# Two chained attention kernels on one core: more turning on TensorE, four experts scored densely in the last two batches

## The chip, the core and the metric

One core of one Trainium2 chip runs the whole program. The metric is the device time of one execution in microseconds (us), median of three.

## What is computed

Eight batches (B), eight heads (H), 512 tokens (S) and 32 state rows (Ns) of 64 numbers (D). First every head lets its tokens read the state and the state read the tokens. The 544 resulting rows, heads side by side, are the input (512 wide) of a mixture of four attention experts, of which each row takes two:

```python
scores = scale * x @ state.T ; xread = softmax(scores) @ state          # per batch and head
scores2 = scale * state @ x.T ; sread = softmax(scores2) @ x
y = concat([xread, sread], axis=2)                                      # -> (8, 544, 512)
topk = two largest of y @ w_gate ; w = softmax over the two
for e in range(4):
    q, k, v = y @ wq[e], y @ wk[e], y @ wv[e]
    ye = softmax(causal(scale * q @ k.T)) @ v @ wo[e]
    out += (w of e where e is chosen, else 0) * ye
```

(The reference pads the rows to 576 in a setup that isn't used; the output has 8 x 544 rows of 512.)

## The kernel before

Nearly all numbers are held as a pair of float16, a high part and the rest, and a product of two such numbers is three float16 matmuls (`PROD`, high by high, high by low, low by high). `hi_lo` (L356) and `split` (L338) make the pairs.

Per batch there are these steps, each a function inside the kernel. `load` (L503) fetches x. `front` (L527) splits x into a float16 pair (`xh`), turns it (`xT`, by a DMA transpose issued on SP's queue; batch 0 turns it on TensorE before the split and splits the turned values), scores it against the state (`bd`), takes the softmax in `eb`, turns that into `at`, folds the state into the weights (`gs`), and from `at` and `gs` makes values `v`, gate logits `lg`, keys `kt` and queries. `gate` (L809) finds the two chosen experts. The queries of a tile of 128 tokens are written twice with masks: one slot holds the chosen lower expert, the other the chosen higher one, each as three experts' columns of which two are zeroed (`qf`); split to `qh`, they are turned by a DMA transpose into `qm`. `side` (L776) does the state's read of the tokens (`e2`, `a`, `a2t`), and every second batch `tail` (L962) handles the 64 state rows of two batches.

`probs` (L843) takes a unit of one or two of the four token tiles: scores of both slots (each three wide matmuls over two experts' 128 rows and three narrow ones over one expert's 64 rows; two narrow ones run side by side in the array), mask and maximum on VectorE (`masked`), exponential on ScalarE, split, and a DMA transpose of the pair (`pt<-ph`). `reads` (L886) multiplies with the values (two slots, three experts each, 193 columns), divides, weights, adds the slots, splits (`zh`), turns by one DMA transpose a tile (`z<-zh`; the last batch's three smaller tiles on TensorE), multiplies with `wo` and sends 128 rows out. Units are `[(0, 1), (2,), (3,)]` for each batch (L1069); a unit is read two units later (`LAG`).

What the code records is not the order on the engines. Every operation becomes a step (`Steps.step`, L175), and `Steps.run` (L256) issues all of them in the order of the table `ORDER`, worked out ahead; the same table holds, for steps that may run on several engines (`either`, L210), which one it is, and which buffer each use takes. So all instructions carry line L266, and only tile names tell them apart. Each engine works through its list in order, and all DMAs are issued by SP, in order too. `FILL` (L19) places 34 matmuls on zeros in the first 15 us (`warm`, L498); their operand is called `band`.

Of the kernel before, what the change touches and what calls it, by code (L numbers as in the profile page):

```python
# [11 lines left out]
F32 = mybir.dt.float32  # L12
# [6 lines left out]
CFG = dict(FILL=(1.0, 1.4, 1.8, 2.2, 2.6, 3.0, 3.4, 3.8, 4.2, 4.6, 5.0, 5.4, 5.8, 6.2, 6.6, 7.0, 7.4, 7.8, 8.2, 8.6, 9.0, 9.4, 9.8, 10.2, 10.6, 11.0, 11.4, 11.8, 12.2, 12.6, 13.0, 13.4, 13.8, 14.2,), RA=-1, RG=1, RV=2, RK=2, ZL=3, GP=1, PT=4, ZM=4, SM=4, QM=4, SIDE=32, FB=1, PX=1, PA=2, LB=1, xn=4, W0=-33, PACE=37.0, LAG=2,  # L19
           FRONT=1.5, FSPAN=1.0, TSPAN=1.3, TOFF=1.2, KT=3, p32=3, ph=2, at=1, et=1, gs=1, xh=4, a2=1, o=4, sn=1, qf=2,  # L20
           n_eb=1, n_e2=1, n_a2t=1, n_xt_tail=2, n_z32=3, n_z=2, n_zh=3, n_tq=1, n_tv=2, n_tpt=2, n_tz=2)
ORDER = (
    (
        "c-jq@gO(5q6acSpwbf>8+ict0X4|%Hd$VoZwr$(Cjraax&Y77ikPPxdQb-B;AQ(zQey9)0p%8>(L)Z-f2m}lQ3I+}tAq(t<RFD<+K_<ussi8"
        "5Xhs=-`!a;b5009sYvO^=-18E=^<bZV00&+u6D2nAV543~|*b17!UFZx~p*3`YI#3tdKqV{z_n-_^g$!^Xib7W?2c_U3Jb<=P3<^LBs09z99"
        "Xy3d5E%j?3PgoIPz}1lV`vYLpgVMczR(Q%!4oKh(I7g+fS3>qVnZB=3-KU6bcCAF1A0Pb>;;{mIF!WU@C*t<b0~{Vp*MuWC3p_?U^EngvhV^"
        "9K^1%nwV^sxf>KxvC%{Rl4A<Zl6vsGp9!lUTNB{{T5hRBGa2Q_0Bp3r@;V7JeBQOHSK}8${17IMWgNYCZAut#g!v#17Q(*>7gCQ^zPQxr157"
        "XfUEP?ef8|J`Sm<#)19$bW_P!89^P?!%3U?D7m)vyM(KxupfTVWe)fMxI&*1;{<4kIBhZG;2x4vxbpsD_(x2W*0>cpJ9iPS^~?U^8yV9XJ`P"
        "<8qh+v1kj{z^!-(8saXfiLG%3G{T+O0ItAF2+zB)7QTnw*ckWVDo6rB@CBM+3fhacu|1}wBy=4vLkDb%!4yOtu?{9A!XHo<Q_**5gJ0nre1M"
        "<u8=7G<`UUkcDgA{26s(Voe;_$E$3(Ob|3L#(bnJwQX+O5W8vmo#8M|Q@Y>5Z3Eq2B3*aKT(KWvBP!7w65;KBF_`r`l$hlug0Cw_+bG!(;Q0"  # L30
# [239 lines left out]
def state_read_then_moe_attention(ctx: ExitStack, tc: tile.TileContext, x, state, w_gate, wq, wk, wv, wo, out):  # L270
# [20 lines left out]
    V0 = 2  # L291
# [105 lines left out]
    def constants():  # L397
# [37 lines left out]
        def ones(v, *rows):  # L435
            for a in range(2):
                fill(v[(slice(None), a, *rows, slice(V0 - 1, V0 + VW + 1, VW + 1))], 1.0 - a)

        vbs = []
        for i in range(CFG["KT"]):  # L440
            vbs.append(st.buf(f"v{i}", [P, 2, T, VW + 4], F16))
            ones(vbs[-1], slice(None))
        tvs = []
        for i in range(CFG["n_tv"]):
            tvs.append(st.buf(f"tv{i}", [P, 2, V0 + VW], F16))
            fill(tvs[-1], 0.0)
            fill(tvs[-1][:NB * NS, 0, V0 - 1:V0], 1.0)
# [42 lines left out]
    tz, e2s = {}, {}  # L490
    xt_tail, kts, vs, qts, wgts, pts, c6s = {}, {}, {}, {}, {}, {}, {}
# [620 lines left out]
```

## Time and profile before

| | us |
|---|---|
| median of 3 runs (lowest, highest) | 292.36 (290.67, 292.72) |
| the profiled execution | 294.35 |
| its span, first to last instruction | 292.6 |
| mean granted TensorE clock | 0.994 of full speed |

The profile describes the one profiled execution, which took 2.0 us more than the median. Engines are PE (TensorE), PEld (its weight loads), DVE (VectorE), ACT (ScalarE), POOL (GpSimd) and SP, which issues the DMAs. In a timeline row the time of a group runs from its first start to its last end, and the end of a matmul lies about 0.17 us behind the start of the next one. So the pace of a group is read from its start to the start of the group that follows.

### The profile page before, as it was taken

What the parts mean: (1) busy time and instruction counts of PE and PEld (TensorE: products, weight loads), DVE (VectorE), ACT (ScalarE), POOL (GpSimd) and SP (SyncE); (2) the same over time, 40 slices, a digit from 0 to 9 for tenths busy, and PEclk for the clock granted to TensorE, in tenths of its full rate; (3) what the DMA queues carried; (4) which work ended last, traced back from release to release, by engine and by line L of the source; (5) the groups of instructions that cost most, each with busy time, mean ns of one, the idle gap of its engine ahead of it and who ended that gap; (6) DMA issues with size and microseconds to landing.
All of it is one profiled execution on the core that took longest, in us unless ns stands there. A gap on an engine that the chain in (4) does not pass through costs nothing.

```text
span 292.6 us, 8929 instructions
## 1 busy us (share of the span) xinstructions
PE 278.0 (95%) x3308; PEld 185.4 (63%) x3311; DVE 245.8 (84%) x771; ACT 223.4 (76%) x604; POOL 168.3 (58%) x242
## 2 busy tenths in 40 slices
PE   7999899989999799999999899999999999999795
PEld 4756555754867457676764758667676677846463
DVE  0797799999999769999999799898988988975481
ACT  3599899898999589889859789986796784376323
POOL 4873646568865578788555884687355750336000
PEclk9999999999999799999999999999999999999999
DMA  6959999998899989989899999999599779558954
GB/s 186 234 123 187 221 191 226 224 216 167 173 176 255 186 182 205 193 195 189 191 203 181 214 179 164 195 190 236 131 176 147 190 137 178 123 108 150 182 202 180
DMA packets 165532, 54.01 MB, mean 185 GB/s; under 512 B 144368, under 2 KB 161008, under 8 KB 165488
## 3 DMA queue, kind: packets, MB, share of 16 engines
q1 hardware_dynamic: 165488, 53.44, 95.2%
q8 instruction: 26, 0.43, 0.6%
q14 instruction: 18, 0.15, 0.2%
HBM read 11.08 MB, written 8.91 MB: 68 GB/s over the span
## 4 chain that ended last, share of the span: by engine, by line
PE 70%; DVE 14%; ACT 8%; DMA 5%; issue 2%; POOL 0%; DVEq 0%; ACTq 0%; SPq 0%
PE bank L266 70%; ACT p L266 2%; DMA a2t<-a 2%; DMA out_dram<-o 2%; DVE qf L266 2%; DMA xn<-in_x_dram 1%; DVE p L266 1%; DVE sbm L266 1%; ACT e L266 1%; DVE ph L266 1%; DVE xh L266 1%; DVE eb L266 1%; DVE m L266 1%; DVE gs L266 1%; ACT at L266 1%
## 5 line engine op out<-in xcount | busy, mean ns | idle before, releaser
L266 PE MATMUL bank<-gs,at 128*128 128x260 f16 (+3 forms) x368 | 50.7, 283 | 0.4
L266 PE MATMUL bank<-wo_n,z 128*128 128x512 f16 (+1 forms) x198 | 46.3, 373 | 1.6 <-ACT z L266 1.6
L266 PE MATMUL bank<-kt,qm 64*128 64x512 f16 (+7 forms) x384 | 45.9, 299 | 0.4 <-DVE gs L266 0.2
L266 PE MATMUL bank<-v,pt 128*128 128x193 f16 x480 | 44.5, 246 | 0.0
L266 PEld LDWEIGHTS <-pt 128*128 128x128 f16 x480 | 39.9, 97 | 4.7 <-issue 1.8
L266 PEld LDWEIGHTS <-at 128*128 128x128 f16 x336 | 31.8, 97 | 8.7 <-issue 1.5
L266 ACT ACTIVATE p<-p,mx 128x384 f32<-128x384 f32 (+3 forms) x64 | 33.4, 555 | 2.9 <-POOL mx L266 2.4
L266 PEld LDWEIGHTS <-qm 128*128 128x128 f16 (+1 forms) x384 | 22.9, 96 | 19.3 <-issue 9.4
L266 POOL TENSOR_TENSOR ph<-p,ph 128x768 f16<-128x768 f32 (+1 forms) x16 | 28.6, 1793 | 9.1 <-ACT lg L266 2.9
L266 DVE CUSTOM_DVE_ANT_0 p<-bank,band 128x256 f32<-128x256 f32 (+3 forms) x64 | 28.9, 481 | 4.9 <-PE bank L266 4.9
L266 PEld LDWEIGHTS <-z 128*128 128x128 f16 x198 | 18.1, 97 | 21.3 <-issue 3.1
L266 ACT ACTIVATE o<-bank 128x512 f32<-128x512 f32 (+1 forms) x28 | 16.0, 583 | 12.4 <-PE bank L266 10.0
L266 PE MATMUL bank<-at,gs 128*128 128x512 f16 (+1 forms) x92 | 24.0, 398 | 0.6 <-DVE xt_tail L266 0.4
L266 ACT ACTIVATE xh<-xn 128x512 f16<-128x512 f32 x32 | 19.4, 625 | 6.5 <-DMA xn<-in_x_dram 3.2
L266 POOL TENSOR_TENSOR zh<-z,zh 128x256 f16<-128x256 f32 x24 | 16.6, 696 | 12.5 <-ACT zh L266 8.7
L266 POOL TENSOR_TENSOR qh<-qf,qh 128x768 f16<-128x768 f32 x10 | 16.6, 1666 | 11.7 <-ACT qh L266 6.3
L266 ACT ACTIVATE ph<-p 128x768 f16<-128x768 f32 (+1 forms) x20 | 18.5, 924 | 0.5 <-DMA pt<-ph 0.4
L266 POOL TENSOR_TENSOR eb<-eb,sbm 128x512 f32<-128x512 f32 x14 | 14.9, 1067 | 6.5 <-DVE sbm L266 4.7
L266 DVE SCALAR_TENSOR_TENSOR xh<-xn,xh 128x512 f16<-128x512 f32 x24 | 16.9, 709 | 0.5 <-ACT xh L266 0.5
L266 PE MATMUL bank<-a2t,xh 128*128 128x64 f16 x384 | 13.5, 198 | 3.2 <-DMA a2t<-a 2.1
L266 DVE TENSOR_TENSOR qf<-bank,m 128x384 f32<-128x384 f32 x28 | 14.8, 549 | 1.8 <-PE bank L266 1.0
L266 PEld LDWEIGHTS <-xh 128*128 128x128 f16 x384 | 13.0, 101 | 4.4 <-DMA a2t<-a 2.4
(217 smaller groups left out, 633.8 us busy)
## 6 DMA issues: line engine op xcount, KB each, us to landing
out_dram<-o SPq DMA_DIRECT2D x33, 256.0 KB, 2.7
xn<-in_x_dram SPq DMA_DIRECT2D x16, 512.0 KB, 4.7
sn<-in_state_dram SPq DMA_DIRECT2D x9, 64.0 KB, 3.8
p<-in_moe_wo_dram SPq DMA_DIRECT2D x2, 256.0 KB, 3.7
z<-zh SPq DMA_TRANSPOSE x29, 2.7
xT<-xh SPq DMA_TRANSPOSE x28, 3.7
p<-in_moe_wv_dram SPq DMA_DIRECT2D x1, 384.0 KB, 5.1
p<-in_moe_wk_dram SPq DMA_DIRECT2D x1, 384.0 KB, 7.6
```

What stands on the lines that cost most here:

```text
L266: f(**{k: v.ap() if isinstance(v, View) else v for k, v in kw.items()})
```

## The change

1. `FILL` has 10 entries for 34.
2. Batch 0's first scores are made in float32: x is turned as before, copied once as float32, and the state's block matrix is float32 too (it lies in the buffer of `et`). 48 float16 matmuls become 16 float32 ones, twice (the tokens' scores and, packed in the array, the state's). x of batch 0 is loaded in four pieces for two, and the second copy of its state is made on the chip.
3. `turn` is new: x of batch 1 (`XP`) and the queries of batch 0 (`QP`) are turned on TensorE (56 turns of 128 x 128) and copied out of PSUM in 8 pieces, for 4 and 2 DMA transposes.
4. Batches 6 and 7 (`D1`, `DA`) score all four experts: no masked queries, the turned queries come straight from a product, 12 narrow score matmuls per tile (two side by side) for 6 wide and 6 narrow, four softmaxes per row for two, 65-column reads of one expert each for 193-column reads of three, and weights of 0 for experts not chosen. A batch then has five units for three, each of 1024 columns.
5. Where both tiles of a unit are read together (batches 0 to 6), their `zh` is one buffer `zhp`, turned by one DMA transpose into `zp`, for two.
6. The high part of a split from SBUF may now run on GpSimd or VectorE, values `v` lie 65 columns apart with a column of ones behind each expert, and buffers are shared or fewer (`n_pt`, `n_tpt`, `n_tz`).
7. `ORDER` is a new table.

```diff
-CFG = dict(FILL=(1.0, 1.4, 1.8, 2.2, 2.6, 3.0, 3.4, 3.8, 4.2, 4.6, 5.0, 5.4, 5.8, 6.2, 6.6, 7.0, 7.4, 7.8, 8.2, 8.6, 9.0, 9.4, 9.8, 10.2, 10.6, 11.0, 11.4, 11.8, 12.2, 12.6, 13.0, 13.4, 13.8, 14.2,), RA=-1,
+CFG = dict(FILL=(1.0, 1.4, 1.8, 2.2, 2.6, 3.0, 3.4, 3.8, 4.2, 4.6,), RA=-1,
...
+XP=(1,), QP=(0,),
...
+n_pt=3, D1=6, DA=6)
...
+    def units_of(b):
+        if b < CFG["D1"]:
+            units = [((0, "s"), (1, "s")), ((2, "s"),), ((3, "s"),)]
...
+        else:
+            units = [((1, "d"),), ((0, "0"), (2, "0")), ((0, "1"), (2, "1")), ((3, "0"),), ((3, "1"),)]
+        return units
...
+    def turn(here, out, in_, n, m):
+
+        if not here:
+            st.dma(out, in_, 0.000875 * n * P, transpose=True)
+            return
+        for k in range(0, n, m):
+            tp = bank("turn").bitcast(F16)[:, :m * P]
+            st.transposes([(tp[:, i * P:(i + 1) * P], in_[:, (k + i) * P:(k + i + 1) * P]) for i in range(m)], identh, 0.055 * m, into=[out[:, k:k + m]])
+            out_of_bank(m * P, out[:, k:k + m].rearrange("p k q -> p (k q)"), tp, 1.0)
...
-                    hi_lo(DM, xT[:, u, 0, 4 * k:4 * k + 4], xT[:, u, 1, 4 * k:4 * k + 4], tp.rearrange("p (h q) -> p h q", q=P), 128.0)
+                    out_of_bank(DM, xT[:, u, 4 * k:4 * k + 4], tp.rearrange("p (h q) -> p h q", q=P), 128.0)
...
-                       for h in range(H) for n, (a, cc) in enumerate(PROD)], (24, 2 * NS, 128, 1), into=[eb])
+                       for h in range(H)], (8, 8 * NS, 128, 1), into=[eb])
...
+        if len(dense) == T:
+            q = qm[:, :4 * T].rearrange("p (a r t) q -> p a r (t q)", a=2, r=2)
+            for pr in range(2):
...
+                    st.mm(chain((pp, gs[:, a, g, cols], at[:, g, c, :]) for g in range(2) for a, c in PROD), (6, S, 128, 1), into=[q[:, :, pr]])
+                hi_lo(S, q[:, 0, pr], q[:, 1, pr], pp, 0.5 ** 15)
...
+        if i in all_experts(b):
+            for s in range(E):
+                to = (s + 1) % E * DW
+                g += chain((zp[:, to:to + DW], rows(s, j)(c), v[:, a, j, s * DW:(s + 1) * DW]) for j in range(i + 1) for a, c in PROD)
...
+                    st.dma(zz.rearrange("p n a r q -> p (n a r) q"), zh.rearrange("p n a c -> p (n a c)"), 0.9, transpose=True)
```

How the order moves, at three places. First SP's queue where it leaves the weights and comes to the first transposes (`xh`, `xT`: x and turned x; `a2t<-a`: the state's softmax; `qm<-qh`: queries; `xn`, `sn`, `p`: loads of x, state and weights). Before:

```order
L266 DMA p_2_114<-in_moe_wk_dram 128x4x64
L266 DMA_TRANSPOSE xT_97<-xh_93 128x8x128
L266 DMA xn_87<-in_x_dram 128x8x128
L266 DMA_TRANSPOSE a2t_151<-a_0_152 128x8x128
L266 DMA_TRANSPOSE xT_97<-xh_93 128x8x128
L266 DMA_TRANSPOSE xT_97<-xh_94 128x8x128 x2
L266 DMA p_2_114<-in_moe_wo_dram 128x512
L266 DMA xn_89<-in_x_dram 128x8x128
L266 DMA_TRANSPOSE a2t_151<-a_0_152 128x8x128
L266 DMA_TRANSPOSE qm_133<-qh_143 128x12x128
L266 DMA sn_85<-in_state_dram 128x2x64
L266 DMA_TRANSPOSE qm_133<-qh_142 128x12x128
```

The same place now:

```order
L266 DMA p_2_114<-in_moe_wk_dram 128x4x64
L266 DMA_TRANSPOSE a2t_151<-a_0_152 128x8x128
L266 DMA p_1_113<-in_moe_wo_dram 128x512
L266 DMA xn_87<-in_x_dram 128x8x128
L266 DMA sn_85<-in_state_dram 128x2x64
L266 DMA_TRANSPOSE a2t_151<-a_0_152 128x8x128
L266 DMA xn_89<-in_x_dram 128x8x128
L266 DMA xn_88<-in_x_dram 128x8x128
L266 DMA sn_85<-in_state_dram 128x2x64
L266 DMA_TRANSPOSE a2t_151<-a_0_152 128x8x128
L266 DMA xn_90<-in_x_dram 128x8x128
L266 DMA_TRANSPOSE xT_97<-xh_96 128x8x128
```

The six transposes of batch 1's x and batch 0's queries are gone from the queue, and the loads and the state's transposes behind them stand sooner.

Second VectorE's list from its third instruction (`xT` here is batch 0's turned x, `bd` the state, `mb` and `eb` the first softmax, `sn` the state as loaded). Before:

```order
L309 CAST identh<-ident 128x128
L266 SCALAR_TENSOR_TENSOR xT_97<-bank_79,xT_97 128x512
L266 SCALAR_TENSOR_TENSOR xT_97<-bank_80,xT_97 128x512
L266 SCALAR_TENSOR_TENSOR bd_0_91<-bank_77,bd_0_91 64x256 x2
L266 SCALAR_TENSOR_TENSOR xT_97<-bank_84,xT_97 128x512
L266 SCALAR_TENSOR_TENSOR xT_97<-bank_78,xT_97 128x512
L266 TENSOR_REDUCE mb_117<-bank_80 128x16
L266 TENSOR_REDUCE mb_117<-bank_84 128x16
L266 TENSOR_TENSOR eb_115<-bank_80,mb_117 128x512
```

Now:

```order
L310 CAST identh<-ident 128x128
L266 TENSOR_SCALAR xh_95<-xn_89 128x512
L266 COPY sn_0_86<-sn_0_86 128x2x64
L266 SCALAR_TENSOR_TENSOR xh_95<-xn_89,xh_95 128x512
L266 TENSOR_SCALAR xT_97<-bank_82 128x512
L266 TENSOR_SCALAR xh_96<-xn_90 128x512
L266 TENSOR_REDUCE mb_116<-bank_83 128x16
L266 TENSOR_TENSOR eb_115<-bank_83,mb_116 128x512
L266 TENSOR_REDUCE mb_116<-bank_81 128x16
```

The six low parts ahead of the first softmax are gone; one copy of turned x and pieces of x's split stand there.

Third SP's queue in the last batch (`pt<-ph`: turned softmax; `z<-zh`, `zp<-zhp`: turned reads; `tpt`: the tail). Before, from its first softmax transpose to its last:

```order
L266 DMA_TRANSPOSE pt_0_163<-ph_156 128x16x128
L266 DMA_TRANSPOSE z_176<-zh_177 128x4x128
L266 DMA_TRANSPOSE pt_0_162<-ph_155 128x12x128
L266 DMA_TRANSPOSE z_175<-zh_179 128x4x128
L266 DMA_TRANSPOSE tpt_203<-ptl_201 128x10x128
L266 DMA out_dram<-o_183 128x512
L266 DMA_TRANSPOSE pt_0_157<-ph_156 128x12x128
```

Now, its last four:

```order
L266 DMA_TRANSPOSE pt_159<-ph_155 128x16x128
L266 DMA out_dram<-o_180 128x512
L266 DMA_TRANSPOSE tpt_202<-ptl_201 128x10x128
L266 DMA_TRANSPOSE z_182<-zh_184 128x4x128
L266 DMA_TRANSPOSE pt_157<-ph_156 128x16x128
L266 DMA_TRANSPOSE pt_158<-ph_155 128x16x128
L266 DMA out_dram<-o_177 128x512
L266 DMA out_dram<-o_178 128x512
L266 DMA out_dram<-o_179 128x512
L266 DMA_TRANSPOSE pt_159<-ph_156 128x16x128
```

The last batch sends five softmax transposes of 16 blocks where it sent three of 16, 12 and 12; the last of them stands behind three outputs.

Over the whole program SP issues 104 transposes for 117, and VectorE's list has 785 rows for 761. Of the 8 copies of turned values out of PSUM, ScalarE has 6 (three of 128 x 1024, three of 128 x 768) and VectorE one of each.

## Rows read from the trace of the kernel before

**Rows 1.** Page, part 1: busy time (share of the span), number of instructions.

```profile
PE 278.0 (95%) x3308; PEld 185.4 (63%) x3311; DVE 245.8 (84%) x771; ACT 223.4 (76%) x604; POOL 168.3 (58%) x242
```

**Rows 2.** Windows: length, busy us of PE PEld DVE ACT POOL, PEclk, DMA share, GB/s.

```profile
0.00:20.20 20.20, 17.59 (x181) 10.44 (x182) 11.74 (x26) 11.79 (x28) 13.51 (x38) 1.00 0.81 193
20.20:40.80 20.60, 18.71 (x275) 12.09 (x278) 17.07 (x48) 18.18 (x48) 10.40 (x20) 1.00 1.06 190
40.80:102.60 61.80, 58.12 (x726) 38.72 (x724) 57.73 (x181) 55.24 (x152) 39.26 (x50) 0.97 1.08 201
...
224.80:262.70 37.90, 37.90 (x375) 25.54 (x369) 32.20 (x119) 23.33 (x66) 16.75 (x22) 1.00 0.73 154
262.70:292.60 29.90, 25.12 (x221) 16.21 (x220) 15.52 (x45) 12.22 (x33) 5.65 (x8) 1.00 0.76 177
```

**Rows 3.** Chain that ended last, in order of time: start, us, what.

```profile
93.49 5.24 DMA a2t<-a
...
163.48 104.06 PE bank L266 x1228
...
273.82 15.65 PE bank L266 x136
```

**Rows 4.** Timeline of PE, 0 to 24 us: start, us, operation, count.

```profile
1.18 3.59 PE L266 MATMUL bank<-band 128*128 128x512 bf16 x8 [1.18 <-DVE band L304]
...
7.25 1.24 PE L266 MATMUL bank<-band 128*128 128x512 bf16 x5
...
9.64 3.32 PE L266 MATMUL bank<-bd,xT 128*128 128x64 f16 x48
12.89 0.86 PE L266 MATMUL bank<-xT,bd 64*32 64x256 f16 x48
...
20.22 2.15 PE L266 MATMUL bank<-gs,at 128*128 128x260 f32 x8
```

**Rows 5.** Groups by form, weight loads and VectorE: count | busy, mean ns.

```profile
L266 PEld LDWEIGHTS bank<-gs,at 128*128 128x128 f32 x32 | 5.7, 190 | 2.0 <-ACT at L266 0.7 <-issue 0.5
...
L266 DVE SCALAR_TENSOR_TENSOR xT<-bank,xT 128x512 f16<-128x512 f32 x4 | 2.6, 686 | 6.3 <-ACT xT L266 6.2
```

**Rows 6.** Timeline of PE, 96 to 103 us.

```profile
98.78 2.54 PE L266 MATMUL bank<-a2t,xh 128*128 128x64 f16 x48 [2.15 <-DMA a2t<-a]
101.25 1.41 PE L266 MATMUL bank<-wn,bd 64*32 64x512 f16 x24
```

**Rows 7.** Timeline of PE, 254 to 271 us.

```profile
254.75 1.57 PE L266 MATMUL bank<-xt_tail,wn 128*128 128x64 f16 x48
256.16 2.21 PE L266 MATMUL bank<-kt,qm 128*128 128x512 f16 x12
...
259.61 1.73 PE L266 MATMUL bank<-kt,qm 128*128 128x384 f16 x12
...
264.10 0.51 PE L266 MATMUL bank<-tk,tq 128*128 128x128 f16 x6
264.44 1.46 PE L266 MATMUL bank<-wo_n,z 128*128 128x512 f16 x6
265.74 1.75 PE L266 MATMUL bank<-kt,qm 128*128 128x128 f16 x24
...
268.73 2.17 PE L266 MATMUL bank<-v,pt 128*128 128x193 f16 x24
```

**Rows 8.** Page, part 5: groups over the whole run, count | busy, mean ns.

```profile
L266 ACT ACTIVATE p<-p,mx 128x384 f32<-128x384 f32 (+3 forms) x64 | 33.4, 555 | 2.9 <-POOL mx L266 2.4
...
L266 DVE CUSTOM_DVE_ANT_0 p<-bank,band 128x256 f32<-128x256 f32 (+3 forms) x64 | 28.9, 481 | 4.9 <-PE bank L266 4.9
...
L266 ACT ACTIVATE ph<-p 128x768 f16<-128x768 f32 (+1 forms) x20 | 18.5, 924 | 0.5 <-DMA pt<-ph 0.4
...
L266 DVE TENSOR_TENSOR qf<-bank,m 128x384 f32<-128x384 f32 x28 | 14.8, 549 | 1.8 <-PE bank L266 1.0
```

**Rows 9.** View of the DMAs: issues, count, median us from issue to landing.

```profile
pt<-ph SPq DMA_TRANSPOSE x24, 4.8
```

More of the change, by code (lines that the diff above doesn't have):

```diff
@@ L508, in load @@
                 twice["sn"] = st.buf("sn2", [P, 2, 2, D])
-                for r in range(2):
-                    st.dma(twice["sn"][:, :, r], state[0].rearrange("(j c) n d -> n j c d", c=2), 0.4)
+                st.dma(twice["sn"][:, :, 0], state[0].rearrange("(j c) n d -> n j c d", c=2), 0.4)
+                kw = dict(out=twice["sn"][:, :, 1], in_=twice["sn"][:, :, 0])
+                st.either([("DVE", 0.2, (nc.vector.tensor_copy, kw)), ("ACT", 0.3, (nc.scalar.activation, dict(**kw, func=AF.Copy, scale=1.0)))])
             else:
@@ new lines, in front @@
+        if len(dense) == T:
+            q = qm[:, :4 * T].rearrange("p (a r t) q -> p a r (t q)", a=2, r=2)
+            for pr in range(2):
+                pp = bank("pp")
+                cols = slice(pr * P, (pr + 1) * P)
+                if whole:
+                    st.mm(chain((pp, gs[:, g, cols], at[:, g]) for g in range(2)), (2, 4 * S + 230, 128, 1), into=[q[:, :, pr]])
+                else:
+                    st.mm(chain((pp, gs[:, a, g, cols], at[:, g, c, :]) for g in range(2) for a, c in PROD), (6, S, 128, 1), into=[q[:, :, pr]])
+                hi_lo(S, q[:, 0, pr], q[:, 1, pr], pp, 0.5 ** 15)
+            for t in range(T):
+                qts[b][t] = q[:, :, :, tok[t]]
@@ L874, in probs @@
-        shifted(2 * nb, mx)
-        for k, i in enumerate(unit):
-            for s in range(2):
-                o = 2 * at_[i] + s * w_[i]
-                act(w_[i], p32[:, o:o + w_[i]], p32[:, o:o + w_[i]], AF.Exp, psum=False, bias=mx[:, 2 * k + s:2 * k + s + 1])
+            for i, how, s, ch, cols, _ in reversed(lanes):
+                r, pr = (hi_, lo_)[s], 1 - s if how == "s" else ch // 2
+                narrow.append((sp[s][:, cols], qs[i][r, a, 1 if how == "s" else pr], kt_[r, c, pr, :P * (i + 1)]))
@@ L879, in probs @@
+        for out, m, scores, w in at:
+            masked(w, out, scores, consts["maskb"][:, DM + P - w:], m)
+        shifted(len(lanes), mx)
+        for out, m, _, w in at:
+            act(w, out, out, AF.Exp, psum=False, bias=m)
         n *= 2
@@ L889, in reads, with rows @@
         z6 = st.buf("z6", [P, 2, 3 * D], F32, bufs=CFG["n_z32"])
+        z32 = z6.rearrange("p s c -> p (s c)")[:, 2 * D:]
+        def rows(s, j):
+            return lambda c: lanes[s][0][:, c, lanes[s][1] + j, :]
         zp = bank("zp")
[L892 removed]
         g = []
[L894 to L896 removed]
@@ L1078, in state_read_then_moe_attention @@
             if k >= CFG["LAG"]:
-                for i in units[k - CFG["LAG"]]:
-                    reads(b, i)
+                left = [i for i, _ in units[k - CFG["LAG"]] if not any(i == i_ for unit in units[k - CFG["LAG"] + 1:] for i_, _ in unit)]
+                if len(left) == 2 and b < B - 1:
+                    zh = st.buf("zhp", [P, 2, 2, E * D], F16)
+                    zz = st.buf("zp", [P, 2, 2, 2, P], F16)
+                    for n, i in enumerate(left):
+                        reads(b, i, zh[:, n], zz[:, n])
+                    st.dma(zz.rearrange("p n a r q -> p (n a r) q"), zh.rearrange("p n a c -> p (n a c)"), 0.9, transpose=True)
+                    for n, i in enumerate(left):
+                        result(b, i, zz[:, n])
+                else:
+                    for i in left:
+                        reads(b, i)
         if b == B - 1:
```

346 lines of the change are left out of this document (199 added, 147 removed).

## Prediction

> **What bounds the kernel now.** I read the shares first, then the windows by stage, the chain of waits, and last TensorE's timeline at three places. TensorE is busy for 278.0 us, 95%, VectorE for 245.8 and ScalarE for 223.4 [rows 1]. The windows say that this means different things in different stages [rows 2]. To 20 us the loads and the first softmax set the pace. From 20.2 to 102.6 us nobody is alone: TensorE idles 1.9 and 3.7 us in the two stretches, VectorE 3.5 and 4.1, ScalarE 2.4 and 6.6, and the DMA engines are full. Behind that TensorE alone decides: the chain of waits is one TensorE run of 104.06 us from 163.48 on, and its last piece is again TensorE, for 15.65 us from 273.82 [rows 3]. In the window from 224.8 it is busy for all of the 37.90 us. In the last two windows together, 67.8 us long, VectorE idles 20.1 us, ScalarE 32.3 and GpSimd 45.4. So a matmul saved after some 102 us is time saved, and work added to the other engines late is nearly free; before 102 us neither is sure.
>
> **Batch 0 and the fills.** Four low parts of 128 x 512 at 686 ns each [rows 5] go from VectorE's list ahead of the first softmax, and x comes in smaller pieces, so that its first turning can begin sooner. On the path are the two scorings, 3.25 us (9.64 to 12.89) and 0.86 [rows 4]. In float32 the first has 16 matmuls for 48. No row shows this form; the nearest is that eight float32 matmuls of 260 columns took 2.15 us, 0.27 each, with weight loads of 190 ns [rows 4, 5]. Bound by these loads, 16 take 3.0 us, so little of the 3.25 goes; what goes is mostly the low parts, 2.7 us of VectorE, half of it beside the matmuls. I take -1.0, between -2.5 (all low parts on the path) and +1.0 (16 at 0.27 us, 4.3).
>
> [...]
>
> The 24 fills taken away cost nothing as work: they ran where TensorE had nothing else. [...]
>
> **Turning on TensorE.** 56 turns of 128 x 128. The nearest row is six matmuls of that size in 0.34 us (264.10 to 264.44) [rows 7], 57 ns each, so 3.2 us of TensorE. They are copied out by ScalarE in six pieces and by VectorE in two. A 128 x 768 or 128 x 1024 copy on ScalarE from SBUF averages 924 ns [rows 8]: 5.5 us of ScalarE and about 2 us of VectorE. All this falls before 102 us, where TensorE idles 5.6 us, ScalarE 9.0 and VectorE 7.6 [rows 2]. If the idle time lies where the turns do, the cost is nothing; if ScalarE is the late engine there, it is up to 5.5. I take +1.3: ScalarE is busy for 18.18 of the 20.60 us in which most of these copies stand, so 3.1 of the 5.5 don't fit there, and somewhat under half of that is not caught up in the next stretch.
>
> **SP's lighter queue.** In exchange six transposes leave SP's queue early, as the first piece of the order shows, and all transposes and loads behind them move up. Before, TensorE waited 2.15 us for the state's transpose `a2t<-a` until 98.78, which had been under way since 93.49 for 5.24 us. Its 48 matmuls then took 2.47 us to 101.25 [rows 3, 6]. The same number of the same shape took 1.41 us at 254.75 to 256.16 [rows 7]; the windows show a granted clock of 0.97 in that stretch and 1.00 elsewhere [rows 2]. So the stall cost 2.15 + 1.06 = 3.2 us in all, and 0.4 more of the next matmuls if they were slow too. A 104-transpose queue for 117 should bring this transpose in time, but a new order has its own late ones: -2.0, between -3.6 and 0.
>
> **VectorE before batch 6.** Its list is 24 rows longer over the program, and part of that stands early (pieces of x's split that ScalarE had, copies of turned values). With 7.6 us idle to 102.6 us I take +0.5, from 0 to +3: all the early additions, about 5 us with the two turn copies, less what these idle times take.
>
> **The dense batches.** Per batch the scores go from 6 wide and 6 narrow matmuls a tile (the narrow ones two side by side, so 9 passes) to 12 narrow, 6 passes. A batch's scores took 2.21, 1.73 and 1.75 us, together 5.69 [rows 7]; 6/9 of it is 3.79, so -1.90. Its reads go from 60 matmuls of 193 columns to 120 of 65. The last 24 of the old form took 2.17 us, of which 0.17 is the tail of the last, 83 ns each: 60 take 5.0. Matmuls of 64 columns took 1.41 us for 48 [rows 7], 29 ns each: 120 take 3.5, so -1.5. The queries have as many columns either way. Two batches give -6.8; I take -6.7. The bounds are -7.3 (65 columns at the pace of the five fast fills of 512, 0.21 us or 0.42 ns a column [rows 4]: 27 ns, reads 3.3 us) and -0.2 (65 columns as slow as the 128 of the turns, 57 ns: reads 6.8 us); the 64-column row is the nearest by far.
>
> What VectorE and ScalarE get for it: masks and maxima of twice as many columns, 8 more at 481 ns, +3.85 us a batch, less four masked queries at 549 ns; exponentials, 8 more at 555 ns, +4.4 us of ScalarE [rows 8]; and GpSimd or VectorE the low parts of two more units. For two batches that is some 8 us of VectorE and 9 of ScalarE into the idle 20.1 and 32.3 us of the last 67.8 [rows 2].
>
> **Waits in the last two batches.** Idle time is not cover by itself: each unit must be masked, exponentiated, split and transposed before it is read. From the end of the last long TensorE run (163.48 + 104.06 = 267.54) to the last one (273.82) such a chain took 6.3 us before, with matmuls lying beside it [rows 3], and a `pt` transpose takes 4.8 us to land [rows 9]. Now five follow one another, and the last stands behind three outputs in SP's queue (third piece of the order). Other matmuls are placed between, so I take +1.4, about a quarter of one such chain; from 0 to +6.3, one whole chain.
>
> **The sum.** -1.0 + 1.3 - 2.0 + 0.5 - 6.7 + 1.4 = -6.5. Against the profiled execution, 294.35 us, that is 287.85. It took 2.0 us more than the median of the runs, so against the median I forecast **285.9 us**. A measurement of this kernel tells about 1%, 2.9 us, from no change: faster is below 289.4, slower above 295.3.
>
> **Rivals.**
>
> *The clock.* The first eight fills took 3.59 us, 0.43 each; five at 7.25 took 1.24, 0.21 each without the tail [rows 4]. [...] Chance 0.08.
>
> [...]
>
> *VectorE and ScalarE set the pace to batch 6.* The early additions, 5 us, come out in full, because these engines idle only in pieces too short to use; TensorE idles more before 102 us, and the dense batches' saving remains. Then 5 us are added to the forecast: 290.9. For it speaks VectorE's 57.73 of 61.80 us; against it that TensorE was still busier, 58.12. Chance 0.12.
>
> *Slower: the last batch's softmax.* Its two extra units each expose the whole chain of 6.3 us, since reads follow in the order of units and outputs share SP's queue: 12.6 for the 1.4 priced, so 285.9 + 11.2 = 297.1. It decides from the point at which waits of TensorE after 225 us exceed 10.8 us (1.4 and the 9.4 from the forecast to 295.3). For it speaks that this tail was bound by just this chain before; against it, 32 us of idle ScalarE and the products with `wo` placed between. Chance 0.14.
>
> *The queue brings nothing.* The transpose is late in any case, because another stands where the old one did: the term of -2.0 goes, and 287.9 results. It lies inside the forecast's own range and is counted with it.
>
> **How the numbers follow.** Forecast 0.66, all of it faster. The clock's 0.08 counts as no change; of the second rival 0.10 is no change and 0.02 faster; the third's 0.14 is slower. So faster 0.68, same 0.18, slower 0.14. The terms' lower ends that can come together (-2.5, -3.6, no late waits) give 281; above, the range takes in both rivals of no change and leaves most of the slower one out: 281.0 to 294.5.
>
> **What would show it.** Right: TensorE's busy time falls by some 7 us, the scores of the last two batches take 3.8 us and reads 3.5 per batch, no wait for `a2t<-a` stands at the first state reads, and the chain stays on TensorE from about 100 us. [...]

## The result and the profile after

The changed kernel takes 284.49 us (median of 4 runs, 283.06 to 284.73), the kernel before 292.53 in the same comparison: 8.0 us less, ratio 0.973, 95% interval 0.968 to 0.978. The forecast was 285.9 us, faster. The profiled execution took 284.73 us, its span is 283.0.

The page's part 1 after, which answers to [rows 1]:

```profile
PE 270.7 (96%) x3406; PEld 182.6 (65%) x3407; DVE 252.9 (89%) x795; ACT 230.5 (81%) x624; POOL 170.2 (60%) x246
```

TensorE is busy for 7.3 us less, and its idle time falls from 292.6 - 278.0 = 14.6 to 283.0 - 270.7 = 12.3 us; together that is the 9.6 us by which the spans differ. Every other engine has more to do, VectorE 7.1 us.

The 7.3 us are not all work saved. The fills (`band`) before and after, then the turns of x and of the queries:

```profile
L266 PE MATMUL bank<-band 128*128 128x512 bf16 x31 | 9.5, 444 | 1.6 <-DVE band L304 1.2 <-issue 0.2
...
L266 PE MATMUL bank<-band 128*128 128x512 bf16 x9 | 4.1, 574 | 1.2 <-DVE band L305 1.2
L266 PE MATMUL bank<-identh,xh 128*128 128x128 f16 x32 | 3.1, 250 | 2.1 <-DVE xh L266 1.9 <-POOL tv L385 0.2
L266 PE MATMUL bank<-identh,qh 128*128 128x128 f16 x24 | 1.8, 220 | 0.0
```

The fills are 5.4 us less, and they stood where TensorE had nothing else; the turns bring in 4.9 us. Without the fills TensorE has 278.0 - 9.5 = 268.5 us of work before and 270.7 - 4.1 = 266.6 after, and 24.1 and 16.4 us without work. So most of what was gained between the two profiled executions, some 7.7 of 9.6 us, is time in which TensorE had no work; what the dense batches save on TensorE, the turns and the float32 scores largely take again.

The windows, with the columns of [rows 2]; the last two are as long as the last two there, counted from the end:

```profile
0.00:20.20 20.20, 16.32 (x158) 11.91 (x159) 11.42 (x26) 12.48 (x28) 10.55 (x39) 0.92 0.82 189
20.20:40.80 20.60, 19.61 (x306) 14.18 (x306) 18.89 (x50) 19.57 (x49) 9.87 (x18) 0.99 0.75 168
40.80:102.60 61.80, 58.87 (x794) 39.92 (x792) 59.51 (x183) 57.46 (x162) 43.51 (x57) 1.00 1.06 185
215.20:253.10 37.90, 37.70 (x525) 23.51 (x521) 35.34 (x129) 29.51 (x67) 19.17 (x30) 1.00 0.88 177
253.10:283.00 29.90, 26.59 (x337) 17.63 (x334) 20.29 (x72) 16.14 (x43) 5.71 (x7) 1.00 0.93 212
```

Three things are to be seen. From 20 to 103 us TensorE idles 3.9 us instead of 5.6, although the turns were put there. In the window from 215.2 TensorE is still full, and VectorE now is nearly so: 35.34 us against 32.20 before. And the first window has a granted clock of 0.92 where it was 1.00.

The long pieces of the chain that ended last, in order of time:

```profile
190.81 40.94 PE bank L266 x515
243.85 35.85 PE bank L266 x462
```

Before, one TensorE run reached from 163.48 to 267.54, and 6.3 us of softmax chain lay behind it [rows 3]. Most of these 6.3 us lay beside matmuls; TensorE waited for the last 1.63 us of them:

```profile
273.82 1.47 PE L266 MATMUL bank<-wo_n,z 128*128 128x512 f16 x6 [1.63 <-ACT z L266]
```

Now one TensorE run carries the chain to the end (243.85 + 35.85 = 279.70), and a mixed stretch of 12 us (231.75 to 243.85) lies ahead of it, among batch 6's dense units.

### The profile page after: what moved, and what is told of

The parts are those of the page before. It is cut to its first block, busy times and chain, and to the rows that moved or that the text cites. A ratio compares the mean times of both kernels' runs of the same rounds, so it can differ in the third digit from the quotient of the medians.

```text
span 283.0 us, 9152 instructions
## 1 busy us (share of the span) xinstructions
PE 270.7 (96%) x3406; PEld 182.6 (65%) x3407; DVE 252.9 (89%) x795; ACT 230.5 (81%) x624; POOL 170.2 (60%) x246
## 4 chain that ended last, share of the span: by engine, by line
PE 68%; DVE 19%; ACT 6%; issue 3%; DMA 2%; SPq 1%; POOL 0%; DVEq 0%; ACTq 0%
PE bank L266 68%; DMA xn<-in_x_dram 2%; DVE eb L266 2%; DVE xh L266 1%; DVE qf L266 1%; DVE sbm L266 1%; DVE gs L266 1%; DVE mb L266 1%; DVE p L266 1%; DVE z L266 1%; DVE a L266 1%; DVE ph L266 1%; SPq L266 1%; DVE m L266 1%; DVE et L266 1%
## 5 line engine op out<-in xcount | busy, mean ns | idle before, releaser
L266 ACT ACTIVATE p<-p,mx 128x256 f32<-128x256 f32 (+3 forms) x80 | 41.8, 554 | 2.8 <-DVE mx L266 1.7
L266 PE MATMUL bank<-v,pt 128*128 128x194 f16 (+1 forms) x600 | 42.1, 226 | 0.5 <-DVE mx L266 0.4
L266 PE MATMUL bank<-kt,qm 64*128 64x128 f16 (+7 forms) x384 | 42.3, 298 | 0.2 <-DVE kt L266 0.2
L266 DVE CUSTOM_DVE_ANT_0 p<-bank,band 128x384 f32<-128x384 f32 (+3 forms) x80 | 36.4, 481 | 0.7 <-PE bank L266 0.3
L266 POOL TENSOR_TENSOR ph<-p,ph 128x1024 f16<-128x1024 f32 (+1 forms) x17 | 32.8, 1930 | 5.7 <-ACT ph L266 5.1
L266 PEld LDWEIGHTS <-qm 64*128 64x128 f16 (+1 forms) x384 | 21.0, 95 | 17.1 <-issue 7.6
L266 PE MATMUL bank<-wo_n,z 128*128 128x512 f16 (+1 forms) x114 | 26.2, 368 | 0.0
L266 ACT ACTIVATE ph<-p 128x1024 f16<-128x1024 f32 (+1 forms) x21 | 20.3, 965 | 0.4
L266 PE MATMUL bank<-wo_n,zp 128*128 128x512 f16 x84 | 19.9, 379 | 0.0
L266 ACT ACTIVATE o<-bank 128x512 f32<-128x512 f32 (+1 forms) x27 | 15.4, 575 | 4.9 <-PE bank L266 2.7
L266 ACT ACTIVATE gs<-bank 128x260 f16<-128x260 f32 (+3 forms) x32 | 15.2, 499 | 1.1 <-PE bank L266 1.1
```

Source lines behind the costliest of these rows:

```text
L266: f(**{k: v.ap() if isinstance(v, View) else v for k, v in kw.items()})
```

## Experiments

All were timed against the kernel before, on several chips; the changed kernel itself, 284.5 us, was timed in the first comparison alone. The kernel before had medians of 291.3 to 292.5 us in the five comparisons, so a difference from the changed kernel is uncertain by about 1.2 us. In the edits `...` marks what is left out; of the table `CFG` only the changed entry is shown, and the re-encoded table `ORDER` is not shown.

### The dense batches

`e4`, TensorE's saved work put back:

```diff
-        st.mm([(*x, h in (begun[0][0], begun[1][0]), h >= len(g) - ended) for h, x in enumerate(g)],
+        again = len(g) // 2 if unit[0][1] != "s" else 0
+        st.mm([(*x, True, False) for x in g[:again]] + [(*x, h in (begun[0][0], begun[1][0]), h >= len(g) - ended) for h, x in enumerate(g)],
...
-            st.mm(g, (len(g), DW, 128, 1), into=[z6])
+            st.mm([(*x[:3], True, False) for x in g[:len(g) * 51 // 120]] + g, (len(g), DW, 128, 1), into=[z6])
```

> The changed kernel; the dense tiles of batches 6 and 7 issue half of their score matmuls and 51 of 120 of their reads a second time (overwritten), which brings TensorE's work there back to that of the kernel before, about 6.8 us in all; all else stays. Theory 'TensorE sets the pace': the time grows by the whole 6 to 7 us, to 290.5 to 291.5. Rival 'softmax sets the pace in the dense batches': part of the added work lies in waits, under 4 us more, below 288.5.

Measured: 290.67 us (289.54 to 292.15), 6.2 more; ratio to the kernel before 0.994 (0.992 to 0.997). TensorE's busy time rose by 5.8 us, and all of it shows. The chain says so in one row: a single TensorE run of 94.89 us to the end.

```profile
190.39 94.89 PE bank L266 x1249
```

`e8` and `e10`, more VectorE work there (`e8`: every mask of a dense unit twice; `e10`: only the first of each unit; the new last argument says how often):

```diff
...
-            masked(w, out, scores, consts["maskb"][:, DM + P - w:], m)
+            masked(w, out, scores, consts["maskb"][:, DM + P - w:], m, 1 if unit[0][1] == "s" else 2)
```

> The changed kernel; each mask-and-maximum of a dense unit is issued twice on VectorE (same result), about 7.7 us more of VectorE in the last two batches. Theory 'covered': VectorE idles there and TensorE has other matmuls between, so under 2 us: 284.5 to 286.5. Rival 'softmax chain': the chain of a unit is on the path and most of it shows: 288 to 292.

> The changed kernel; in each dense unit only the first mask-and-maximum is issued twice: 10 for 32 in the run before, 4.7 us of VectorE (per batch 0.68 twice, 0.42 and 0.28 twice). Theory 'VectorE is full there': two thirds or more of it shows, 287.5 to 289.5. Rival 'a little room': VectorE's idle 13 us of the last 83 take most of it, 284.5 to 286.5, and only the larger addition overflowed.

Measured: `e8` 299.99 us (ratio 1.030, 1.024 to 1.035), 15.5 more. The edit was larger than its expectation says: a dense batch has 16 masks, not 8, so 32 more at 481 ns, 15.4 us; VectorE's busy time rose from 252.9 to 267.8. `e10` took 288.31 us (0.990, 0.987 to 0.993): 3.8 more for 4.7 us of masks by its expectation (VectorE's busy time rose by 4.2). So about four fifths or more of what is added to VectorE in these batches shows, also where it is little.

The profiles say where. The last batch's `a2t,xh` matmuls, a place that all these orders share, in the changed kernel, `e7` (below) and `e10`:

```profile
214.78 1.56 PE L266 MATMUL bank<-a2t,xh 128*128 128x64 f16 x48
...
214.69 1.56 PE L256 MATMUL bank<-a2t,xh 128*128 128x64 f16 x48
...
212.82 1.56 PE L266 MATMUL bank<-a2t,xh 128*128 128x64 f16 x48
```

`e10` is 2.0 us early there and 2.0 us late at the end (285.0 for 283.0): the last stretch takes 72.2 us for 68.2. Up to about 1 us of the 4.0 may be what any early arrival loses at the end (`e1`, below).

What TensorE waits for longest in `e8` (us in total, times, longest), and its windows:

```profile
PE bank L266 <- DVE mx L266: 6.9, 6, 2.3
```

```profile
230.00:245.00 15.00, 11.25 (x64) 5.98 (x62) 14.14 (x53) 9.33 (x21) 3.21 (x7) 0.89 0.49 97
245.00:260.00 15.00, 12.03 (x186) 8.01 (x186) 14.29 (x45) 9.38 (x21) 5.87 (x9) 1.00 0.69 146
```

VectorE is at 94 to 95% and TensorE at 75 to 80%: `mx` is the maximum that the doubled masks deliver. In the first of the two windows the granted clock fell to 0.89 as well, so a part of the 15.5 us may be the clock's; how much is not shown.

`e12`, VectorE relieved: the engine chosen for three low parts (`ph`) of batch 6 in the table is GpSimd for VectorE, no line of code changes.

> The changed kernel with three low parts of turned softmax of batch 6 (1.23 us each, at 230 to 239 us) moved from VectorE to GpSimd, 3.7 us of VectorE less; order as it is. Theory 'both are full': TensorE has no idle time from 200 to 260 us either, so relieving VectorE alone brings nothing: 284 to 285.5. Rival 'VectorE alone is the bound': 1.5 to 3.5 us faster, 281 to 283.

Measured: 286.32 us (284.64 to 287.94), not faster, if anything slower; ratio 0.982 (0.978 to 0.986). VectorE had 2.2 us less to do, and the time did not follow. GpSimd took 2.13 us for a low part that VectorE did in 1.23, and the three end 1.2, 1.7 and 2.0 us later than in the changed kernel, so each unit's transpose starts later. So `e12` lengthens the chain that it relieves, and does not show by itself what less VectorE work would bring. The changed kernel's own trace bounds it: from 214 us to its last matmul TensorE waits once, for 0.2 us.

```profile
PE bank L266 <- DVE kt L266: 0.2, 1, 0.2
```

Together with `e4`, `e8` and `e10`: TensorE and VectorE are both nearly full in the dense batches, and additions to either show. Whether less TensorE work alone would still bring something was not tried.

### Turning on TensorE

`e3` puts all six DMA transposes back, each at the place of its turn in the order; `e6` has only the line of `XP`.

```diff
-XP=(1,), QP=(0,),
+XP=(), QP=(),
```

> The changed kernel with the six transposes of batch 1's x and batch 0's queries back on SP's queue, each where its first turn stood. Theory 'queue': what the turns cost TensorE (3.2 us of work) is less than what the DMA path costs (waits of TensorE up to 60 us some 4 us shorter than before): 1 to 3 us slower, 285.5 to 287.5. Rival 'turns are only work': TensorE has 3.2 us less to do and waits no more: 1 to 3 us faster, 281.5 to 283.5.

> The changed kernel with only batch 1's x back on DMA transposes; batch 0's queries stay on TensorE. Theory 'queries': all that the run without any turns lost came from the queries (a wait of 3.9 us and the slow clock behind it); x's turns save no wait and cost 1.8 us of work, so 283 to 285. Rival 'both': half of the 6.7 us comes back, 287 to 289.

Measured: `e3` 291.19 us (289.57 to 292.74; ratio 0.997, 0.994 to 1.000), 6.7 more than the changed kernel. `e6` 286.24 us (285.65 to 287.74, five executions; 0.984, 0.979 to 0.989), 1.8 more. So the turns of x are worth some 1.8 us and those of the queries 4.9, in this order; counted from the kernel before in each comparison, 2.9 and 4.2. The chain of `e3` shows why:

```profile
38.61 5.20 DMA qm<-qh
```

and TensorE's timeline the price:

```profile
43.86 3.18 PE L256 MATMUL bank<-kt,qm 128*128 128x128 f16 x24 [3.92 <-DMA qm<-qh]
46.97 0.84 PE L256 MATMUL bank<-wn,bd 64*32 64x512 f16 x24
```

TensorE waits 3.92 us for the queries' transpose, and its next 24 matmuls take 3.11 us, where the changed kernel's take 1.68 (from 40.60 to 42.28 us of its timeline): 5.4 us at one place. The granted clock is 0.50 from 44 to 46 us in `e3`, and 1.00 from 38 to 43 us in the changed kernel.

`e5` does the turns alone in the kernel before, each where its DMA stood:

```diff
-            st.dma(qm[:, 2 * u:2 * u + 2].rearrange("p t a k q -> p (t a k) q"), qh.rearrange("p t a c -> p (t a c)"), 1.34, transpose=True)
+            turn(b in (0,), qm[:, 2 * u:2 * u + 2].rearrange("p t a k q -> p (t a k) q"), qh.rearrange("p t a c -> p (t a c)"), 12, 6, 1.34)
```

and the same for batch 1's x.

> The kernel before (292.1 us) with the turns alone: batch 1's x and batch 0's queries are turned on TensorE and copied out, each where its DMA transpose stood in the order; nothing else moves. Theory 'depends on the order': in the old order other matmuls lie between a query's transpose and its scores, so the turns save no wait there and only TensorE's 3.2 us of work and the copies come in, partly into idle time: 291.5 to 294. Rival 'turns are worth 6 us': what the run without turns lost (291.2 for 284.5) is what they bring in any order: 286 to 288.

Measured: 301.58 us (301.10 to 302.83), ratio 1.037 (1.033 to 1.041): some 10 us slower, beyond both theories. Most of it is lost early: the first `a2t,xh` matmuls start at 47.11 us for 38.98 in the kernel before. In its timeline:

```profile
34.24 1.13 PE L257 MATMUL bank<-gs,at 128*128 128x256 f32 x4 [1.11 <-ACT xT L257]
...
43.19 1.98 PE L257 MATMUL bank<-at,gs 128*128 128x512 f32 x4 [1.71 <-ACT qm L257]
```

A turn stands in TensorE's own list and its copy in ScalarE's, where the DMA transpose stood in SP's. These two waits of TensorE end with such a copy (`xT`, `qm`); together they are 2.8 us, and for the rest of the loss no single wait stands out. VectorE's windows fall to 12.23 and 14.44 of 20 us from 20 to 60, for 16.47 and 18.90, and the granted clock is 0.95 and 0.96 there, for 1.00. In the two orders tried, the turns pay only in the one that was made with them.

### Start and end

`e2` takes 24 of the 34 fills from the kernel before.

```diff
-FILL=(1.0, 1.4, 1.8, 2.2, 2.6, 3.0, 3.4, 3.8, 4.2, 4.6, 5.0, 5.4, 5.8, 6.2, 6.6, 7.0, 7.4, 7.8, 8.2, 8.6, 9.0, 9.4, 9.8, 10.2, 10.6, 11.0, 11.4, 11.8, 12.2, 12.6, 13.0, 13.4, 13.8, 14.2,)
+FILL=(1.0, 1.4, 1.8, 2.2, 2.6, 3.0, 3.4, 3.8, 4.2, 4.6,)
```

> The kernel before (292.5 us) with its last 24 fills taken out and nothing else. Theory 'clock': the fills that stood at 14 to 19 us held the clock; without them it is at half somewhere between 14 and 22 us, and the time grows by 1.5 to 4 us (294 to 296.5). Rival 'idle work': the fills only stood where TensorE had nothing to do; clock 1.00 as before, time within 0.7 us of 292.5.

Measured: 290.81 us (12 runs; ratio 0.997, 0.993 to 1.000), 1.3 faster: neither theory. The clock did fall:

```profile
17.50:20.90 3.40, 3.01 (x11) 2.58 (x12) 3.33 (x9) 2.78 (x7) 2.94 (x12) 0.54 0.56 105
```

That stretch stood behind a wait of 2.36 us, and it cost about 1 us there (the `ident,eb` and `gs,at` matmuls took 4.38 us to their next neighbour for 3.32); yet the second half of x was turned 0.9 us sooner, so that `gs,at` began at 19.69 for 20.22 us. That turn waited for x's load in both, so whether the fills had to do with it is not shown. And the 2.15 us wait for `a2t` was gone: the transpose, issued at 93.34 us (93.49 before), landed by 96.6.

`e1` puts nine more fills into the changed kernel's wait, ahead of the third turn of x in `ORDER`:

```diff
-FILL=(1.0, 1.4, 1.8, 2.2, 2.6, 3.0, 3.4, 3.8, 4.2, 4.6,)
+FILL=(1.0, 1.4, 1.8, 2.2, 2.6, 3.0, 3.4, 3.8, 4.2, 4.6, 50.0, 51.0, 52.0, 53.0, 54.0, 55.0, 56.0, 57.0, 58.0,)
```

> The changed kernel (284.5 us) with nine more matmuls on zeros in front of the third turn of x, in TensorE's wait at 15.1 to 17.0 us. Theory 'clock': the wait let the granted clock fall to half from 17.0 to 20.6 us, on the path; with the nine it stays at full level, the gs,at products start at about 19.5 for 21.1 us, and the time falls by 1 to 2 us (282.5 to 283.5). Rival 'caught up': VectorE sets the pace from 55 to 90 us, so an earlier start is lost again; the clock is full but the time is within 0.5 us of 284.5.

The stretch that it was to mend, in the changed kernel:

```profile
17.05 0.54 PE L266 MATMUL bank<-identh,xh 128*128 128x128 f16 x4 [1.94 <-DVE xh L266]
17.52 1.11 PE L266 MATMUL bank<-p,bd 64*32 64x256 f32 x16
...
21.13 1.04 PE L266 MATMUL bank<-gs,at 128*128 128x260 f32 x4
```

```profile
17.00:20.50 3.50, 3.45 (x48) 2.76 (x50) 2.73 (x9) 2.89 (x11) 0.78 (x2) 0.52 0.20 46
```

The granted clock is 0.52 there, behind 1.94 us without work. In `e1` it is 1.00 throughout, and `gs,at` begins at 19.22 us, 1.9 sooner; 0.56 of that is there ahead of the fills, since the first scores already begin at 8.01 us for 8.57. The time: 284.56 us (284.01 to 284.96), no change.

What the clock costs here can be read from `e10`, whose start is the changed kernel's, without added fills. In its profiled execution the mean granted clock of the whole span is 0.999 (0.994 in the changed kernel), and behind a like wait stand:

```profile
16.38 0.40 PE L266 MATMUL bank<-identh,xh 128*128 128x128 f16 x4 [1.83 <-DVE xh L266]
...
19.10 2.83 PE L266 MATMUL bank<-gs,at 128*128 128x260 f32 x12
```

From the third turn to `gs,at` it took 2.72 us, the changed kernel 21.13 - 17.05 = 4.08: with the granted clock of 0.52 it took 1.4 us longer, and with the 0.67 us by which its first scores were early (7.90 us) that makes the lead of 2.0 us that `e10` still had at 212.82 us.

In `e1` too the start was won and the end gave it back. The lead was 1.5 us as late as 268 us (the reads at 269.89 stand at 268.34) and shrank to 0.9 behind this wait, and to about 0.5 in the spans (282.5 for 283.0):

```profile
273.70 0.91 PE L257 MATMUL bank<-v,pt 128*128 128x65 f16 x24 [0.46 <-DMA pt<-ph]
```

The last softmax transpose lands too late for the earlier reads, as the rival on the last batch had it. So with the nine fills the clock was at 1.00, and the gain did not outlast the order of the last transfers.

`e11` adds to `e1` an earlier place for that transpose, ahead of two outputs in SP's queue, and two low parts on GpSimd. SP's order there:

```diff
 L266 DMA out_dram<-o_177 128x512
+L266 DMA_TRANSPOSE pt_159<-ph_156 128x16x128
 L266 DMA out_dram<-o_178 128x512
 L266 DMA out_dram<-o_179 128x512
-L266 DMA_TRANSPOSE pt_159<-ph_156 128x16x128
```

> The changed kernel with the nine fills in the wait (as the first run had), two low parts of x's split moved from VectorE to GpSimd at 15 to 18 us, and in the last batch the last softmax transpose moved ahead of two of the three outputs in SP's queue. If the 1.5 us won at the start were lost at the end to that transpose alone, they now remain: 282.5 to 283.8. If VectorE is what holds the last batches, the time stays within 0.5 us of 284.5.

Measured: 285.89 us (285.09 to 287.89), slower than the changed kernel by 1.4. The wait moved to ScalarE, which needs a buffer that the delayed outputs hold:

```profile
273.35 0.60 ACT L257 ACTIVATE o<-bank 128x512 f32<-128x512 f32 x1 [5.52 <-DMA out_dram<-o]
273.84 0.38 ACT L257 ACTIVATE z<-bank 128x256 f16<-128x256 f32 x1
```

and TensorE waits 2.32 us for that `z`. (This profiled execution took 287.89 us, 2.0 over its median, so the size of the wait is not the median's.) With three changes in one run, what each did to the time is not shown; the trace shows that the place of the three outputs mattered. No version tried is faster than the changed kernel.

`e7` makes batch 0's scores in float16 again: pairs for the turned x and the state, three matmuls for one.

```diff
-                    out_of_bank(DM, xT[:, u, 4 * k:4 * k + 4], tp.rearrange("p (h q) -> p h q", q=P), 128.0)
+                    hi_lo(DM, xT[:, u, 0, 4 * k:4 * k + 4], xT[:, u, 1, 4 * k:4 * k + 4], tp.rearrange("p (h q) -> p h q", q=P), 128.0)
...
-                       for h in range(H)], (8, 8 * NS, 128, 1), into=[eb])
+                       for h in range(H) for n, (a, cc) in enumerate(PROD)], (24, 2 * NS, 128, 1), into=[eb])
```

> The changed kernel with batch 0's first scores as 48 float16 matmuls again, twice, with the six low parts on VectorE behind the high parts; loads in four pieces and all else stay. The prediction's term: float32 is worth 1.0 us with the smaller loads, so 285 to 286. Rival 'float32 costs': the float32 scores took 3.8 us for 3.2 in float16, and the low parts hide behind loads: 283.5 to 284.5.

Measured: 286.01 us (285.57 to 288.45; ratio 0.984, 0.979 to 0.988), 1.5 more. But its profile, of an execution of 286.31 us, doesn't put this at the start, although the granted clock fell over the scores themselves (0.50 from 10.90 to 14.30 us, 0.91 over the first 20 us): `gs,at` begins at 21.22 us for 21.13, and the last `a2t,xh` at 214.69 for 214.78 (above). The 1.6 us by which its span is longer are lost behind 267 us, to TensorE's waits for `z` (0.40) and `o` (0.54) and the end. And the float32 scores themselves are not faster. In the changed kernel's trace each float32 matmul of the scores has two records, 32 for the 16:

```profile
8.57 1.97 PE L266 MATMUL bank<-et,xT 128*128 128x64 f32 x16
10.38 0.38 PE L266 MATMUL bank<-band 128*128 128x512 bf16 x1
10.59 1.89 PE L266 MATMUL bank<-et,xT 128*128 128x64 f32 x16
12.42 1.09 PE L266 MATMUL bank<-xT,et 64*32 64x256 f32 x32
```

That is 3.85 us for the first scores with a fill among them, where 48 float16 matmuls took 3.25 [rows 4].

### The kernel before, once more

> The kernel before, unchanged, profiled once more. If TensorE's wait for the state's transpose (2.15 us, and the slow matmuls behind it) belongs to the kernel, it stands here again near 97 us; if it was an accident of the first profiled execution, which took 2.0 us more than the median, it is absent, and the prediction counted it twice: as a term and as the distance to the median.

It took 291.97 us. The same stretch as [rows 6]:

```profile
98.60 1.57 PE L266 MATMUL bank<-a2t,xh 128*128 128x64 f16 x48 [2.12 <-DMA a2t<-a]
100.10 0.84 PE L266 MATMUL bank<-wn,bd 64*32 64x512 f16 x24
```

The wait belongs to the kernel. The slow matmuls behind it don't: 48 in 1.50 us here at a granted clock of 1.00 (95.60 to 103.00 us), in 2.47 there at 0.55 (98.80 to 101.30 us). (This is one execution, and has no median.) Its groups (part 5) give the two that the dense batches change, and below them the changed kernel's:

```profile
L266 PE MATMUL bank<-kt,qm 64*128 64x512 f16 (+7 forms) x384 | 45.9, 299 | 0.4 <-DVE gs L266 0.2
L266 PE MATMUL bank<-v,pt 128*128 128x193 f16 x480 | 44.5, 246 | 0.2
```

```profile
L266 PE MATMUL bank<-v,pt 128*128 128x194 f16 (+1 forms) x600 | 42.1, 226 | 0.5 <-DVE mx L266 0.4
L266 PE MATMUL bank<-kt,qm 64*128 64x128 f16 (+7 forms) x384 | 42.3, 298 | 0.2 <-DVE kt L266 0.2
```

## Why the prediction was right, and where it was not

**Direction and size.** Right: 8.0 us were measured for 6.5 forecast against the median. Of the terms, only that of the dense batches is borne out by itself; those for waits, turning, queue and start are off or not shown, and their errors partly cancel, so that the sum came this close is in part luck. The sign that it named, TensorE's busy time down by some 7 us, came true (7.3), in a sum that it had not made: 6.0 from the dense batches and 5.4 from the fills, less 4.9 for the turns.

**Dense batches (-6.7).** Right in size: scores and reads fell by 3.6 + 2.4 = 6.0 us, and putting the work back cost 6.2. The path there is TensorE's, as forecast.

**"Work added to the other engines late is nearly free."** Wrong as a reading, though it did no harm here; it is the step that failed. It read 20.1 us of idle VectorE in the last 67.8 as room. Most of it lay behind the last mask of the kernel before, which ends at 268.71 us; behind it only the split (`ph`) of one unit is left of the softmax work. Idle there: 23.89 - 10.87 = 13.0 us.

```profile
268.71:292.60 23.89, 19.11 (x167) 12.95 (x166) 10.87 (x32) 8.37 (x25) 2.43 (x6) 1.00 0.74 186
```

The change put 7.9 us more on VectorE in its last 67.8 us, as forecast (some 8), and filled it to 35.34 of 37.90 us in the window from 215.2. That still fitted. Of the next 4.7 us 3.8 show (`e10`).

**Waits in the last two batches (+1.4).** Mis-sized, and of the other sign: in the last 67.8 us TensorE idles 0.20 + 3.31 = 3.5 us, where it idled 4.8. The 6.3 us of the old chain were never exposed whole; TensorE waited 1.63 us for it, and that wait is gone. The slower rival's mechanism exists but did not decide: TensorE's chain is unbroken from 243.85 us to the end. It showed as soon as TensorE came 1.5 us earlier (`e1`).

**VectorE before batch 6 (+0.5), and its rival.** The additions came: VectorE is busy for 3.6 us more from 20 to 103 us. But TensorE idles less there, 3.9 us for 5.6, not more as the rival had it. No run tests the term alone.

**Turning and SP's queue (+1.3 and -2.0).** Mis-sized, and not to be priced apart from the order. In the new order the turns are worth some 7 us, in the old one they cost some 10. The prediction looked for the gain at the state's transpose near 97 us; `e3` shows it where the first scores wait for the queries, near 40 us. There the old order had other matmuls in between, and its TensorE has no wait for `qm`. The wait at 97 us did go: the `a2t,xh` matmuls at 96.25 us follow without one. But its cost was about 2.1 us, not 3.2, since the granted clock of 0.55 behind it was that execution's (1.00 in `e9`). That the lighter queue took the wait away is not shown: in `e2` it went with the old queue.

**Distance to the median.** The profiled execution's 2.0 us held that clock of 0.55, so part of the -2.0 of the queue was subtracted a second time with the step to the median. Between the profiled executions the change was -9.6, for -6.5 forecast.

**Start (-1.0).** Not shown. The prediction priced 16 float32 matmuls with the time of single records, of which each has two (32 in the trace); the scores took 3.85 us, not 3.0. `e7` is 1.5 us slower without float32, but its profile doesn't place that at the start. The start as a whole is not earlier: the chain's `gs,at` begins at 21.13 us for 20.22, because x's turns stand in it with a wait of 1.94 us and a granted clock of 0.52 behind it.

**Fills.** "They cost nothing" was wrong by 1.3 us in the old kernel (`e2`, 0.1 to 1.9 by its interval). The clock, a rival with a chance of 0.08, did fall with ten fills: behind the scores in `e2` (0.54 from 17.50 to 20.90 us) and in the changed kernel (0.52 from 17.00 to 20.50 us), over the float16 scores in `e7` (0.50 from 10.90 to 14.30 us). In `e10`, with the same ten, its mean over the whole span is 0.999. In the changed kernel the matmuls up to `gs,at` took 1.4 us longer than in `e10`. The run with nine more fills was at 1.00, which brought nothing in the median (`e1`).

**What stays open.** The single undoings add up to more than the change: 6.2 (dense) + 6.7 (turns) = 12.9 us against 8.0. A part taken out of an order that was made with it can cost more than it brought, as `e5` shows from the other side, so they are not shares of the gain. The paired transposes of z and the moved high parts were not tried alone, and what the float32 scores are worth is open. Why `a2t` lands earlier without the late fills is not settled.

## What to carry to other kernels

Idle time of an engine is room only where the dependent work can stand: read it per window, and leave out what lies behind the last operation of that kind. A transfer replaced by work on compute engines puts its waits into the lists of those engines, so it may need a new order, and its worth can't be read from the old one. A lead won at the start is kept only if the last transfers of the program are early enough to use it. And a fall of busy time is not yet a gain: count apart what only filled waits.

## What was not expected of the hardware

In the changed kernel TensorE's granted clock was 0.52 over the 3.50 us shown, behind a wait of 1.94 us, although TensorE was busy for 3.45 of them. In the first profile of the kernel before it was 0.55 from 98.80 to 101.30 us, behind a wait of 2.15 us. But it was 1.00 from 95.60 to 103.00 us in the repeated run, with a wait of 2.12 us among them; and in `e10`, whose mean is 0.999, the matmuls of the first place took 2.72 us for 4.08, behind a wait of 1.83 us. The same transpose `a2t<-a`, issued at 93.3 to 93.5 us from the same queue, let TensorE go on at 98.78, 98.60 and, in `e2` with fewer fills ahead, no later than 96.62 us.
